# Two convolutions and a joint layer on one core: the order of the first loads, a split first tap and a wider leading tile

## The chip, the core and the metric

The kernel runs on one core of one Trainium2 chip. The metric is the device time of one execution in microseconds. A core has TensorE (PE) for matmuls, with its weight loads shown apart (PEld), VectorE (DVE), ScalarE (ACT), GpSimd (POOL) and SyncE (SP), which issues the DMA loads and stores of this kernel. Sixteen DMA engines move the data. Each engine runs its own instructions in order; semaphores tie them together.

## The reference

```python
B, T, D, K = 2, 4000, 512, 5          # x: (B, T, D); w1, w2: (K, D, D); g: (B, 8, D)
xp = jnp.pad(x, ((0,0),(pad,pad),(0,0)))
for i in range(K):
    h = h + jnp.einsum("btc,cd->btd", xp[:, i:i+T, :], w1[i])
h = _gelu(h)[:, ::2, :]
...                                    # the same with hp = pad(h) and w2
f = _gelu(f)[:, ::2, :]
fe = jnp.einsum("btd,de->bte", f, w_f)
ge = jnp.einsum("bud,de->bue", g, w_g)
j = jnp.tanh(fe[:, :, None, :] + ge[:, None, :, :])
return jnp.einsum("btud,dv->btuv", j, w_o)
```

Two convolutions of five taps, each with a GELU and a stride of 2, take 4,000 time steps to 1,000. Then every step is paired with 8 vectors of g, and the tanh of the sums goes through a last matmul. All data are bf16. Since only every second output of the first convolution is kept, an output column needs even samples for the even taps (0, 2, 4) and odd samples for the odd taps (1, 3).

## The kernel before, in words

**The leading tile.** The first 2 x NA output columns of the first convolution (NA = 216, line 328) are computed directly, tap by tap. Their samples come untransposed by `load_xr` (line 445) in two loads, one of 128 rows and one of NA + 2 - 128 = 90 rows; a row is four samples of 512 channels, 4,096 bytes. PE transposes them (line 501) into four PSUM banks, and four copies bring them into `xs`: DVE copies those of the first load, ACT those of the second. `direct(i, m)` (line 683) then runs one tap's 4 matmuls for one group of 128 output channels: 2 x NA = 432 columns each. The taps are taken in the order 0, 4, 2, 1, 3: 5 x 4 x 4 = 80 matmuls. They accumulate in PSUM banks 0 to 3, and a GELU on ACT ends them (line 693). Eight matmuls on zeros (`NWARM`, line 491) run on PE before the transposes.

**The triples.** The rest of the first convolution, and all of the second, is done in `Triple` (line 554): a fast scheme that makes three outputs from nine products, in place of more in the direct way. Its inputs are sums and differences of six phases of x (tiles `xq` and `xp`, loaded transposed by `load_x6`, line 449), made by DVE and ACT into `row`, and sums of the weights (`w1part`, line 534), made by DVE and ACT into `w_t` and `w_x`. The first triple's matmuls have N3 = 262 columns, and so have the second's; the others have 334. The leading tile has 72 triple positions of the 334 per batch (NA / 3), and the first two triples 131 each.

**What sets the order.** `Plan` (line 68) collects the operations. Up to line 694 they are pinned, so that each engine takes them in the order in which they are written. Behind that a list scheduler orders DVE and ACT by its own costs, among what is ready; PE, SP and POOL keep the written order among what is ready. Semaphore waits follow from the tiles that an operation reads and writes. `o.after` adds a wait by hand.

**SP's queue.** All loads stand on SP: xr (two), tap 0 of w1 in two halves by output columns (512-byte runs), taps 4, 2, 1 and 3 of 512 KB each, then the transposed loads of xq (twelve), of xp, and so on. Line 469 makes a w1 load wait until the load three places before it in the list `came` has landed. The transposed loads stand behind these waits.

**Weights on DVE.** `w1part(0)` begins with the first operation on w1 that the profile shows on DVE; it reads taps 0 and 4. The fourth operation on DVE reads tap 2, and the tenth taps 1 and 3 (line 543). The `row` operations of the first triple follow, and wait for the first two loads of xq.

The functions that the diff touches follow.

Of the kernel before, what the change touches and what calls it, by code (L numbers as in the profile page):

```python
# [7 lines left out]
ACT = mybir.ActivationFunctionType  # L8
# [4 lines left out]
P = 128  # L13
# [37 lines left out]
class Psum:  # L51
# [6 lines left out]
    def pair(self, lo, step, n):  # L58
        ap = self.h[:, lo:lo + 2 * step].rearrange("p (s c) -> p s c", s=2)[:, :, 0:n]
        cells = np.unique(np.concatenate([np.arange(lo, lo + n), np.arange(lo + step, lo + step + n)]) // 512)  # L60
        return View(ap, cells, True)
# [240 lines left out]
def bass_standalone__seq2seq_rnn_t_joint__speech_kernel(  # L302
# [33 lines left out]
    NWARM = 8  # L336

    with ExitStack() as es:
# [33 lines left out]
        xq = [Buf(nc, f"xq{i}", [6, NK, 288], BF16, v.end - v.bytes) for i, v in enumerate((xs[1], w2_sb))]  # L372
# [46 lines left out]
        def mm(o, pairs, start, stop, check=True):  # L419

            def fn(e):
                for n, (l, r) in enumerate(pairs):
                    ins = e.matmul(o.ap, lhsT=l.ap, rhs=r.ap, start=start and n == 0,  # L423
                                   stop=stop and n == len(pairs) - 1, skip_group_check=not check)
                return ins
            pl.op("pe", fn, [v for pr in pairs for v in pr], (o,), len(pairs) * max(o.ap.free_size() / 2400 + 0.0025, 0.1))
# [18 lines left out]
        def load_xr(rt):  # L445
            n = NR[rt]
            dst = xr[rt].rows(0, n).map(lambda a: a.rearrange("p r k c -> p (r k c)"))
            src = x[0, 4 * P * rt:4 * (P * rt + n), :].rearrange("(p r) c -> p (r c)", r=4)
            return pl.dma("sp", lambda e: e.dma_start(dst.ap, src), (), (dst,), nbytes=n * 4 * 2 * D)

        def load_x6(buf, b, ph, j0, col, n=336):
# [4 lines left out]
            pl.dma("sp", lambda e: e.dma_start_transpose(out=dst.ap, in_=src), (), (dst,), nbytes=n * 2 * D, rate=170e3)  # L456

        came = [load_xr(rt) for rt in range(2)]
        act(warm[0:1], warm[1:2], ACT.Gelu_apprx_tanh)

        def load_w1(i):
            src = w1[i].rearrange("(k c) d -> c k d", c=P)
            if len(came) == 2:
                h = D // 2
                for sl in (slice(0, h), slice(h, D)):
                    o = pl.dma("sp", lambda e, sl=sl: e.dma_start(w1_sb[i, :, sl].ap, src[:, :, sl]), (), (w1_sb[i, :, sl],), nbytes=262144)
            else:
                o = load_w("sp", w1_sb[i], src)
                o.after.append(came[-3].idx)
            came.append(o)  # L470

        def load_xq(i, ph):
            load_x6(xq[i], 0, ph, 2 * NA // 3 + i * N3 - 2, 0, -(-(N3 + 3 - i) // 16) * 16)

        for kind, i in (('w', 0), ('w', 4), ('w', 2), ('w', 1), ('w', 3), ('x', 4), ('x', 0), ('x', 2), ('x', 1), ('x', 3), ('x', 5)):
            if kind == "w":
                load_w1(i)
            else:
                load_xq(0, i)
        for ph in (4, 0, 2, 1, 3, 5):  # L480
            load_xq(1, ph)
# [8 lines left out]

        warm_mm(NWARM)
        psb = ps.h[:, :].bitcast(BF16)
        for rt in range(2):
            for pp in range(2):
                bk, n = 4 + 2 * pp + rt, NR[rt]
                pv = View(psb[:, bk * 1024:(bk + 1) * 1024].rearrange("p (r k c) -> p r k c", r=2, k=NK)[:, :, :, 0:n], np.array([bk]), True)

                def fn(e, rt=rt, pp=pp, pv=pv, n=n):
                    for r in range(2):
                        for k in range(NK):  # L500
                            ins = e.transpose(pv.ap[:, r, k, :], xr[rt].h[0:n, 2 * r + pp, k, :], ident.h[0:n, 0:n])
                    return ins
                pl.op("pe", fn, (xr[rt].rows(0, n), ident[:]), (pv,), 0.55)
                o = xs[0][pp::2, :, 16 + rt * P:16 + rt * P + n]
                if rt:
                    act(o, pv, ACT.Copy)
                else:
                    pl.op("dve", lambda e, o=o, pv=pv: e.tensor_copy(out=o.ap, in_=pv.ap), (pv,), (o,), vec_cost(o, (pv,)))
# [152 lines left out]
        trip = [Triple(xq[0], 2, row[0], wa, to_h(0, j3, N3), N3), Triple(xq[1], 2, row[1], wa, to_h(0, j3 + N3 // 2, N3), N3),  # L661
# [5 lines left out]
        for b in range(B):  # L667
            memset(hT[b][4:6, :, HOFF - 1:HOFF])
            memset(hT[b][:, :, HOFF + NT3:HOFF + NT3 + 2])
        memset(xq[1][0:4, :, 1 + N3:4 + N3])  # L670
        memset(xq[1][4:6, :, N3:4 + N3])
# [4 lines left out]
        def both(i, k):  # L676

            a, b = (xs[0][r, k, 16 + d:16 + d + NA] for r, d in tap_at[i])
            lo, hi = a.ap, b.ap
            ap = bass.AP(tensor=lo.tensor, offset=lo.offset, ap=[list(lo.ap[0]), [hi.offset - lo.offset, 2], [1, NA]])  # L680
            return View(ap, np.union1d(a.cells, b.cells), False)

        def direct(i, m):
            mm(ps.cols(m * NT, 2 * NA), [(w1_sb[i, k, m * P:(m + 1) * P], both(i, k)) for k in range(NK)],
               i == taps[0], i == taps[-1])

        for i in taps:
            for m in range(NK):
                direct(i, m)
        for m in range(NK):  # L690
# [436 lines left out]
```

## Time and profile before

| | us |
|---|---|
| median of 3 runs | 253.12 (252.08 to 253.51) |
| span of the profiled execution, first to last instruction | 251.3 |
| PE busy in the span | 245.7 (98%) |
| DVE busy | 211.8 (84%) |
| ACT busy | 210.5 (84%) |

The span is that of one profiled execution; its time by the clock of the runs is not listed by itself, and the median of the runs is 1.8 us above the span. "Busy" of PE counts matmuls that overlap in its pipeline, so the distance between two starts says more than the length of one.

The first loads, from the trace's records of issue and landing (us from the start of the span):

| load | issued | landed |
|---|---|---|
| xr, 128 rows | 0.74 | 4.17 |
| xr, 90 rows | 1.19 | 5.86 |
| w1 tap 0, two halves | 1.69, 2.14 | 6.61, 7.44 |
| w1 tap 4 | 4.19 | 8.94 |
| w1 tap 2 | 5.88 | 10.44 |
| w1 tap 1 | 7.46 | 12.42 |
| w1 tap 3 | 8.96 | 14.40 |
| xq, first and second of twelve | 9.37, 11.51 | 15.49, 17.94 |

In the first 10 us PE ends its transposes' stream at 6.93 and starts the direct taps at 7.47, when the copies of the even samples are there. In the profile a line such as `7.47 14.81 PE L423 MATMUL ...` gives the start, the length, the engine, the line of the kernel (L423 is the helper `mm`, L410 the helper `tt`, L456 the transposed load), what is written and read, and in brackets the idle time before it with what ended it.

### The profile page before, as it was taken

Reading aid. Unit: us, or ns where it says so; the run is one execution under the profiler, and the core shown is the slowest. Engines: PE = TensorE matmul, PEld = TensorE weight load, DVE = VectorE, ACT = ScalarE, POOL = GpSimd, SP = SyncE. Lnnn points to the kernel's source line nnn. Section 1 sums busy time; section 2 is a strip of 40 time slices with the busy share of each in tenths; the row PEclk is TensorE's granted clock in tenths of the full one; section 3 lists DMA queues with packets and bytes.
Section 4 is the critical chain, followed back from the end, with each engine's and each line's share of the span. In section 5 each row is a group of like instructions: output and inputs, shape, how many; then the busy total and the mean of one; then the engine's idle time right before and its main releaser. Section 6 shows DMA issues by size and latency. Waiting matters only on the chain.

```text
span 251.3 us, 5205 instructions
## 1 busy us (share of the span) xinstructions
PE 245.7 (98%) x1920; PEld 184.6 (73%) x1920; DVE 211.8 (84%) x347; ACT 210.5 (84%) x353; POOL 106.7 (42%) x109
## 2 busy tenths in 40 slices
PE   8999999999999999999999999999999999999994
PEld 4556788877666666666467878777788888778873
DVE  1699999967999997971547798999999999999892
ACT  2388699878959869963799999999999999997763
POOL 1000000000000000003338899698998999699930
PEclk9999999999999999999999999999999999999999
DMA  7999999988400052000002223322344336534648
GB/s 212 326 174 176 186 156 208 176 144 274 148 0 3 0 182 71 1 1 3 0 1 85 83 86 127 127 86 83 127 132 164 128 120 219 187 123 148 207 137 266
DMA packets 57392, 31.92 MB, mean 127 GB/s; under 512 B 33837, under 2 KB 57149, under 8 KB 57367
## 3 DMA queue, kind: packets, MB, share of 16 engines
q1 hardware_dynamic: 57367, 31.59, 48.0%
q8 instruction: 15, 0.25, 0.4%
q14 instruction: 10, 0.08, 0.1%
HBM read 7.71 MB, written 16.38 MB: 96 GB/s over the span
## 4 chain that ended last, share of the span: by engine, by line
PE 85%; DMA 6%; DVE 5%; ACT 2%; SPq 1%; issue 1%; DVEq 0%
PE acc L423 85%; DMA xq<-in_x_dram 3%; DMA w_sb<-in_w_dram 2%; DVE row L410 2%; DMA xr<-in_x_dram 1%; DVE xq L410 1%; SPq L456 1%; ACT sn L843 1%; DVE og L410 0%; ACT jT L415 0%; DVE sn L844 0%; DVE ssum L511 0%; ACT ost L843 0%; DVE w_t L410 0%; DVE w_x L410 0%
## 5 line engine op out<-in xcount | busy, mean ns | idle before, releaser
L410 DVE TENSOR_TENSOR og<-acc,sn 128x512 bf16<-128x512 f32 x87 | 56.9, 681 | 3.9 <-PE acc L423 3.1
L415 ACT ACTIVATE jT<-feT,geT 128x1000 bf16<-128x1000 f32 (+6 forms) x56 | 51.7, 975 | 0.5 <-DVE feT L736 0.4
L423 PE MATMUL acc<-tw,ss 128*128 128x256 f16 x348 | 48.0, 273 | 0.0
L912 POOL TENSOR_TENSOR ss<-jT 128x512 f16<-128x512 bf16 x28 | 33.8, 1219 | 12.9 <-ACT jT L415 10.6
L423 PEld LDWEIGHTS acc<-tw,ss 128*128 128x128 f16 x348 | 33.5, 98 | 7.3 <-DVE sn L844 0.3
L843 ACT ACTIVATE sn<-acc 128x512 f32<-128x512 f32 x52 | 31.5, 620 | 3.5 <-PE acc L423 3.2
L423 PE MATMUL acc<-row,w_sb 128*128 128x334 bf16 (+1 forms) x192 | 33.1, 295 | 0.2 <-DVE row L410 0.2
L423 PE MATMUL acc<-wo_sb,jT 128*128 128x256 bf16 (+1 forms) x196 | 31.7, 288 | 0.0
L407 POOL MEMSET hT<- 128x8 bf16 (+2 forms) x6 | 0.7, 148 | 71.8 <-ACT hT L415 66.8
L423 PE MATMUL acc<-row,w_x 128*128 128x262 bf16 (+1 forms) x192 | 28.2, 290 | 0.0
L415 ACT ACTIVATE jX<-feT,geT 128x1000 bf16<-128x1000 f32 (+4 forms) x28 | 25.0, 932 | 0.0
L423 PEld LDWEIGHTS acc<-row,w_sb 128*128 128x128 bf16 x192 | 18.5, 98 | 6.8 <-DVE row L410 0.5
L423 PEld LDWEIGHTS acc<-wo_sb,jT 128*128 128x128 bf16 x196 | 19.2, 98 | 5.3
L423 PEld LDWEIGHTS acc<-row,w_x 128*128 128x128 bf16 x192 | 18.8, 98 | 5.4
L415 ACT ACTIVATE sd<-acc 128x334 f32<-128x334 f32 (+1 forms) x48 | 20.5, 431 | 1.9 <-PE acc L423 1.3
L912 POOL TENSOR_TENSOR ss<-jX 128x512 f16<-128x512 bf16 x18 | 20.9, 1176 | 1.2 <-ACT jX L415 0.7
L415 ACT ACTIVATE hT<-acc 128x262 bf16<-128x262 f32 (+2 forms) x36 | 15.1, 432 | 6.7 <-PE acc L423 6.6
L511 DVE SCALAR_TENSOR_TENSOR acc<-acc,sd 128x334 f32<-128x334 f32 (+1 forms) x24 | 11.6, 483 | 10.4 <-PE acc L423 10.3
L844 DVE COPY sn<-acc 128x512 f32<-128x512 f32 x25 | 16.9, 682 | 2.4 <-PE acc L423 2.2
L423 PE MATMUL acc<-wo_sb,ss 128*128 128x256 bf16 x116 | 17.9, 273 | 0.0
L423 PE MATMUL acc<-hT,w_sb 128*128 128x334 bf16 x96 | 17.4, 305 | 0.0
L912 POOL TENSOR_TENSOR ss<-ss,jT 128x512 f16<-128x512 f16 x14 | 16.4, 1181 | 0.7 <-PE acc L423 0.4
(105 smaller groups left out, 501.6 us busy)
## 6 DMA issues: line engine op xcount, KB each, us to landing
out_dram<-og SPq DMA_DIRECT2D x44, 256.0 KB, 2.3
w_sb<-in_w_dram SPq DMA_DIRECT2D x9, 512.0 KB, 5.0
out_dram<-og SPq DMA_DIRECT2D x14, 128.0 KB, 2.7
out_dram<-ost SPq DMA_DIRECT2D x7, 128.0 KB, 2.0
xr<-in_x_dram SPq DMA_DIRECT2D x1, 512.0 KB, 3.4
w_sb<-in_w_dram SPq DMA_DIRECT2D x2, 256.0 KB, 5.1
wf_sb<-in_w_f_dram SPq DMA_DIRECT2D x1, 512.0 KB, 3.6
wg_sb<-in_w_g_dram SPq DMA_DIRECT2D x1, 512.0 KB, 4.7
```

Source lines behind the costliest of these rows:

```text
L407: pl.op("pool", lambda e: e.memset(v.ap, 0.0), (), (v,))
L410: pl.op(eng, lambda e: e.tensor_tensor(out=o.ap, in0=a.ap, in1=b.ap, op=op), (a, b), (o,), 0.02 + 2.14e-3 * o.ap.free_size() if eng == "po ...
L415: pl.op("act", lambda e: e.activation(o.ap, i.ap, func, scale=scale, bias=0.0 if bias is None else bias.ap), rd, (o,), o.ap.free_size() * ...
L423: ins = e.matmul(o.ap, lhsT=l.ap, rhs=r.ap, start=start and n == 0, stop=stop and n == len(pairs) - 1, skip_group_check=not check)
L456: pl.dma("sp", lambda e: e.dma_start_transpose(out=dst.ap, in_=src), (), (dst,), nbytes=n * 2 * D, rate=170e3)
L511: pl.op(eng, lambda e: e.scalar_tensor_tensor(out=o.ap, in0=a.ap, scalar=f, in1=b.ap, op0=ALU.mult, op1=add), (a, b), (o,), vec_cost(o, (a ...
L843: pl.flex({"act": (lambda e: e.activation(o.ap, v.ap, ACT.Copy), 0.05 + n * 0.833e-3), "dve": (lambda e: e.tensor_copy(out=o.ap, in_=v.ap) ...
L844: "dve": (lambda e: e.tensor_copy(out=o.ap, in_=v.ap), 0.065 + n * 1.04e-3)}, (v,), (o,))
L912: fn = lambda e, o=S[i], x=x, y=y, op=op: e.tensor_tensor(out=o.ap, in0=x.ap, in1=y.ap, op=op)
```

## The change

- `load_xr` is split by even and odd samples: each load takes two of the four samples of a row, in 1,024-byte runs. The order on SP becomes: even samples of the first rows, tap 0 in halves by input channels (1,024-byte runs), even samples of the second rows, tap 4, odd samples of both, taps 2, 1 and 3, and then the transposed loads as before. The waits by `o.after` are now: tap 2 for tap 4, tap 1 for the first odd samples, tap 3 for the second odd samples.
- NA is 228 in place of 216, so the second xr loads have 102 rows and the direct matmuls 456 columns; N3 is 258 in place of 262 for both triples.
- Tap 0 is done in two column parts (128 and 100 of each of the two interleaved output sets), and the first part in two halves of the input channels. Each part's accumulation covers both sets with `Psum.pair`.
- The transposes are taken apart in `turn`: those of the first even samples follow 5 warm-up matmuls and are followed by one more; those of the second even samples stand after the first 8 matmuls of tap 0; those of the odd samples stand between taps 4 and 2. DVE copies the even samples, ACT the odd ones.
- The memsets of hT and xq move in POOL's written order, and the planner's cost of a short matmul is lower (0.06 for 0.1 us).

The core of the diff (its changes to `Psum.pair` and to the sizes of xq are left out):

```diff
-    NA, N3 = 216, 262
+    NA, N3 = 228, (258, 258)
...
-    NWARM = 8
+    NWARM = 5
...
-        def load_xr(rt):
+        def load_xr(rt, pp):
             n = NR[rt]
-            dst = xr[rt].rows(0, n).map(lambda a: a.rearrange("p r k c -> p (r k c)"))
-            src = x[0, 4 * P * rt:4 * (P * rt + n), :].rearrange("(p r) c -> p (r c)", r=4)
-            return pl.dma("sp", lambda e: e.dma_start(dst.ap, src), (), (dst,), nbytes=n * 4 * 2 * D)
+            dst = xr[rt].rows(0, n, slice(pp, 4, 2)).map(lambda a: a.rearrange("p r k c -> p r (k c)"))
+            src = x[0, 4 * P * rt:4 * (P * rt + n), :].rearrange("(p r) c -> p r c", r=4)[:, pp::2, :]
+            return pl.dma("sp", lambda e: e.dma_start(dst.ap, src), (), (dst,), nbytes=n * 2 * 2 * D)
...
+        def load_w1(i, parts=1):
+            n = NK // parts
+            for k in range(0, NK, n):
+                src = w1[i, k * P:(k + n) * P].rearrange("(k c) d -> c k d", c=P)
+                dst = w1_sb[i, k:k + n]
+                o = pl.dma("sp", lambda e, dst=dst, src=src: e.dma_start(dst.ap, src), (), (dst,), nbytes=n * 131072)
+                if len(came) > 4:
+                    o.after.append(came[-3].idx)
+                came.append(o)
+
+        came = [load_xr(0, 0)]
+        load_w1(0, 2)
+        came.insert(2, load_xr(1, 0))
         act(warm[0:1], warm[1:2], ACT.Gelu_apprx_tanh)
...
+        load_w1(4)
+        for rt in range(2):
+            came.append(load_xr(rt, 1))
+        for i in (2, 1, 3):
+            load_w1(i)
...
+        def turn(rt, pp, eng):
+            bk, n = 4 + 2 * pp + rt, NR[rt]
...
+            def fn(e):
+                for r in range(2):
+                    for k in range(NK):
+                        ins = e.transpose(pv.ap[:, r, k, :], xr[rt].h[0:n, 2 * r + pp, k, :], ident.h[0:n, 0:n])
+                return ins
...
         warm_mm(NWARM)
...
+        turn(0, 0, "dve")
+        warm_mm(1)
...
+        for q0, n in ((0, P), (P, NA - P)):
+            for ks in ((0, 1), (2, 3)):
+                for m in range(NK):
+                    mm(ps.pair(m * NT + q0, NA, n), [(w1_sb[0, k, m * P:(m + 1) * P], both(0, k, q0, n)) for k in ks],
+                       q0 == 0 and ks[0] == 0, False, False)
+                if q0 == 0 and ks[0] == 0:
+                    turn(1, 0, "dve")
+        for i in taps[1:]:
+            if i == 2:
+                turn(0, 1, "act")
+                turn(1, 1, "act")
+            for m in range(NK):
+                direct(i, m)
```

More of the change, by code (lines that the diff above doesn't have):

```diff
@@ L371, in bass_standalone__seq2seq_rnn_t_joint__speech_kernel @@
         assert all(xp[i].end <= xs[i].end for i in xp)
-        xq = [Buf(nc, f"xq{i}", [6, NK, 288], BF16, v.end - v.bytes) for i, v in enumerate((xs[1], w2_sb))]
+        XQ = [-(-(N3[i] + 3 - i) // 16) * 16 for i in range(2)]
+        xq = [Buf(nc, f"xq{i}", [6, NK, XQ[i] + 16], BF16, v.end - v.bytes) for i, v in enumerate((xs[1], w2_sb))]
         assert xq[0].end <= xs[1].end and xq[1].end <= w2_sb.end
@@ L669, in bass_standalone__seq2seq_rnn_t_joint__speech_kernel @@
             memset(hT[b][:, :, HOFF + NT3:HOFF + NT3 + 2])
-        memset(xq[1][0:4, :, 1 + N3:4 + N3])
-        memset(xq[1][4:6, :, N3:4 + N3])
-        tap_at = {0: ((2, -1), (0, 0)), 1: ((3, -1), (1, 0)), 2: ((0, 0), (2, 0)),
-                  3: ((1, 0), (3, 0)), 4: ((2, 0), (0, 1))}
-        taps = (0, 4, 2, 1, 3)
[L676 to L689, printed above, removed]
         for m in range(NK):
```

69 lines of the change are left out of this document (30 added, 39 removed).

## The prediction, on record before the changed kernel ran

> **What bounds the kernel now.** I read the page's chain first: what ends last, and from when. Its header, and then its first 30 us as the chain view gives them (start, length, what):
>
> ```profile
> PE 85%; DMA 6%; DVE 5%; ACT 2%; SPq 1%; issue 1%; DVEq 0%
> ```
>
> ```profile
> 0.74 3.43 DMA xr<-in_x_dram
> 4.17 0.02 issue
> 4.19 4.75 DMA w_sb<-in_w_dram
> ...
> 9.37 2.09 SPq L456
> 11.46 0.05 issue
> 11.51 6.42 DMA xq<-in_x_dram
> 17.94 0.02 issue
> 17.96 1.29 DVE row L410 x2
> ...
> 28.17 0.61 DVE row L410
> 28.78 0.05 issue
> 28.83 185.64 PE acc L423 x1464
> ```
>
> From 28.83 us on TensorE (PE) is the bound without a break for 185.64 us. Before that the chain does not run through PE: it goes through loads (xr, w1, the second transposed load of xq, landing at 17.94) and then through VectorE (DVE), which makes the operands of the triples. The change touches only what happens before 28.83 us and the size of some later matmuls. So the question is when DVE now lets PE go. The timeline of PE and DVE in that stretch (start, length, engine, line, operation):
>
> ```profile
> 1.19 3.60 PE L423 MATMUL acc<-zero 128*128 128x512 bf16 x8 [1.19 <-DVE zero L430]
> 7.47 14.81 PE L423 MATMUL acc<-xs,w_sb 128*128 128x432 bf16 x80 [0.54 <-ACT xs L415]
> 8.97 0.69 DVE L511 SCALAR_TENSOR_TENSOR ssum<-w_sb 128x512 f32<-128x512 bf16 x1 [1.96 <-DMA w_sb<-in_w_dram]
> 10.78 0.68 DVE L511 SCALAR_TENSOR_TENSOR ssum<-w_sb,ssum 128x512 f32<-128x512 bf16 x1
> 17.96 0.70 DVE L410 TENSOR_TENSOR row<-xq 128x1048 bf16<-128x1048 bf16 x1 [0.43 <-DMA xq<-in_x_dram]
> 28.83 0.62 PE L423 MATMUL acc<-row,w_sb 128*128 128x262 bf16 x4 [0.20 <-DVE row L410]
> ```
>
> DVE starts on w1 when tap 4 has landed (8.97), needs tap 2 first in the operation at 10.78, and from there to 17.53 it runs 11 operations back to back, one per 0.605 us. It idles 0.43 us for xq, then works without a pause to 28.78. PE, in contrast, is nearly level: 80 matmuls from 7.47 to 22.12 (0.183 us apart), then 56 of 262 columns at 0.1105 us, to 28.35, then it waits for DVE. An earlier start of the direct taps is therefore worth next to nothing by itself: DVE's chain must come earlier too.
>
> **Own time.** The span is 251.3 us and the median of the three runs 253.12, so 1.8 us lies around it. I make the sum as a shift of the span and add it to 253.12.
>
> **Part 1, the start on PE.** xr's first load lands at 4.17 with 8 packets of 4,096 B per DMA engine, 0.16 us each in the packet records. The even half is half of that: 0.64 us earlier, 3.55. Five warm-up matmuls at 0.427 us end at 3.3. The 8 transposes and the copy took 4.58 to 6.37 in before (5.675 + 0.69); moved to 3.65 they end at 5.44. PE starts tap 0 at 5.45, not 7.47: 2.0 us earlier. Its work from there: 16 matmuls of 256 columns, 16 of 200 and 64 of 456, at 0.183 us scaled by columns (0.109, 0.085, 0.1935): 15.5 us; 24 transposes now behind the start, at the 0.056 and 0.044 us that they show once fast: 1.15 us. 5.45 + 16.65 = 22.1, as now (22.12). The earlier start is eaten by 24 more columns in every matmul and by the transposes. The 56 matmuls then end at 28.3 at best.
>
> **Part 2, the loads.** This is where the time goes. The trace's packet records end each load in 4-byte packets, one per engine that it ran on: the 128-row xr load has 16, the 90-row one 15. The output stores, of 8 to 128 rows, have 1,486 in all, exactly the sum of each one's largest divisor of its rows up to 16; 16 each would be 1,552. With the tile at 228 columns the second xr load has 102 rows (2 x 3 x 17): its two halves go through **6 engines**, 34 packets of 1,024 B each, against 13 if all 16 shared them.
>
> The price of a packet: tap 4 lands at 8.94, tap 2 at 10.44, so 32 packets per engine in 1.5 us, 0.047 us each (the next two loads took 2.0 us each, 0.062, the other end). On those six engines, in queue order from xr's even half at 3.55: tap 0's halves 16 packets each, 4.3 and 5.05; xr1 even 34, 6.65; tap 4 32, 8.15; xr0 odd 8.9; xr1 odd 10.5; tap 2 12.0; tap 1 13.5; tap 3 15.0. The gap from last packet to landing grows from 0.5 us in the first load to 0.75 in the next, so add 0.25: tap 4 8.4 (now 8.94), **tap 2 12.25 (now 10.44)**, tap 3 15.25 (now 14.40). The other ten engines run dry meanwhile: SP holds tap 2 until tap 4 has landed.
>
> No row tells which six engines. Ends: the same six twice (68 packets where 26 would be even, 42 x 0.047 = 2.0 us behind), or two different sixes (half of it). I take the same six, since nothing in the records moves on from load to load, and keep the other as a rival.
>
> The Trainium skill, DMA: Bandwidth & Descriptors, section "Why a DMA increments its semaphore by 16 and not by 1", says that a load uses the largest count up to 16 that divides both sides' slowest dimension, and on the hardware queues always the lowest-numbered engines. The first half agrees with the 15 and the 1,486 above; the second half no row shows. By it both halves sit on the same six, the end I took.
>
> **Part 3, SP.** Tap 3 is now issued behind a wait for xr1's odd half (10.75 landed). Behind it on SP stand all transposed loads: xq's first issue goes from 9.37 to 10.75 + 0.4 = 11.15, 1.8 us later, and its second landing from 17.94 to 19.75. Lower end: that load's issue took 2.8 us where most took 1.6; if it sheds this, 18.55.
>
> **Part 4, DVE.** Its operation at 10.78 now waits for tap 2, 12.27; 11 operations later it is 19.0 (tap 3, needed at 15.9, is there). The first row operation starts at the later of 19.0 and xq (18.55 to 19.75): 19.0 to 19.75 against 17.96; I take **+1.6** (19.55), nearer to the unshortened issue. From there to PE's release stand the same 18 operations, 12 of them 1.5% narrower (about 0.01 us each): -0.1. Release at 28.83 + 1.5 = 30.3. PE would be there at 28.75 (22.1, plus 0.5 waiting for xr1 even, which lands at 6.9 when PE is ready at 6.3, plus 56 x 0.110).
>
> ScalarE now does the odd copies (0.77 + 0.69 us) between weight work; the third doubled row, behind one 1.04 us weight copy, ends near 22.7, before DVE asks for it at 23.2. Cost nothing; without that cover at most 0.5. The unpinned order behind is otherwise the same up to swaps of neighbours, and the moved memsets fill tiles that trip 1 and the second convolution read after 30 us: nothing.
>
> **Part 5, later matmuls.** Triples 0 and 1 have 288 matmuls of 258 columns in place of 262; 232 come after the release: 232 x 4 columns x 0.42 ns (0.183 us / 432) = -0.4 us, straight off the bound.
>
> **Sum:** +1.6 - 0.1 - 0.4 = **+1.1 us, 254.2**; by the ends +0.5 to +2.0 (slow packets), 253.6 to 255.1.
>
> **Rivals.**
> - *The loads are spread evenly* (not slower). 13 packets per xr1 half: tap 4 7.4, tap 2 10.25, xr1 odd 8.75, xq's issue 9.15. DVE passes 10.25 where it stood at 10.78, ends at 17.0 and waits for xq at 17.7: -0.25 - 0.1 - 0.4 = -0.75, **252.4**. It decides if tap 2 lands before 10.8. Against it: 102 has no divisor from 7 to 16, and the store counts. Chance 0.12.
> - *Two different sixes.* Tap 2 near 11.7, xq's issue near 10.1: +0.7 - 0.5 = **253.3**. Chance 0.11.
> - *PE stays slow for longer.* Row: matmuls in before start 0.427 us apart, transposes 0.107, until 5.86, and from there at twice the pace, 4.7 us after the first matmul, with PE never idle (the page's granted clock reads full all along and does not show this). In after PE idles at 3.3 to 3.6 and 4.9 to 5.45. Each slow us costs 0.5; PE has 1.6 us of cover under DVE (28.75 to 30.3) and 0.5 in the wait for xr1, so it decides once the slow pace lasts 4.2 us longer, to 10.1. If counting starts anew at 5.45 it ends at 10.15: hidden. If it lasts until 13: 3.6 - 2.1 = +1.5, **255.7**. Chance 0.15.
>
> The Trainium skill, TensorE: Matmul & The Clock Gate, Part 1, says that PE runs at half rate until one free-running window of about 3.4 us was busy. The 4.7 us agree. By it the pace doubles between 8.9 and 12.3 if the idle spots spoil the windows before: nothing at the one end, +1.1 at the other.
>
> **Numbers.** Forecast 0.62, the rivals 0.12, 0.11, 0.15. Half a per cent, about what a measurement of this kernel can tell from no change, is 1.27 us: 251.85 to 254.39. Of the forecast's 0.62 (253.6 to 255.1, spread by the runs' own 1.4 us) 0.29 lie above; with the third rival and a trace of the second that is 0.46 slower. Faster: a good half of the even-spread case, 0.07. Within: 0.47. Range: below, it reaches into the even-spread case, 252.6; above, to the slow-PE case, 255.9.
>
> **What would show it.** Right: tap 0's first matmul near 5.5; the first DVE operation on w1 near 8.4, its fourth waiting for w_sb until about 12; xq's first issue near 11; row operations from about 19.5; PE's unbroken stretch from about 30.3. Wrong: xq's first issue before 10 (the loads were spread), or matmuls of 456 columns still 0.38 us apart after 10 us (PE slow).

## The result, and the profile after

| | before | changed |
|---|---|---|
| median of 7 runs each, us | 253.12 (252.08 to 253.79) | 256.38 (254.58 to 257.15) |
| ratio of the two | | 1.0121, 95% interval 1.0095 to 1.0147 |
| profiled execution: its time, span | -, 251.3 | 254.67, 252.9 |

The change makes the kernel 3.3 us slower. The forecast was 254.2, and the range ended at 255.9: the sign of the sum was right, its size was not. The profiled execution is one of the two fastest of the changed kernel: its 254.67 us lie inside the forecast's range, and its trace shows less of the loss than a usual run has. Part of the difference is visible: before's trace has some 0.9 us of stalls on PE at 214 to 222 us that this one lacks. Of the 18 traces of the experiments below, 16 have these stalls too (all but those of kernels 9 and 15), so a usual run of the changed kernel probably has them; no trace shows it. From 54 to 210 us (in before's time), ahead of these stalls, every matmul of the changed kernel comes 2.86 to 2.89 us later than its counterpart in before, the matmuls counted from the end. The start, which the trace does show, thus makes up 2.9 of the 3.3 us.

The chain of waits of the changed kernel (header, then start, length, what):

```profile
PE 95%; DMA 2%; SPq 1%; ACT 0%; issue 0%
```

```profile
2.63 5.90 DMA xr<-in_x_dram
8.53 0.04 issue
8.57 0.86 PE acc L504 x8
9.43 6.43 PE acc L425 x40
15.86 0.81 PE acc L504 x16
16.67 233.36 PE acc L425 x1848
```

In before this chain ran through loads and DVE until 28.83 us. Now it is one load and then PE alone: the second even samples land at 8.53, and from 8.57 on nothing but PE holds the end. The timeline of PE, and then of DVE:

```profile
5.71 1.05 PE L425 MATMUL acc<-xs,w_sb 128*128 128x256 bf16 x8 [0.57 <-DVE xs L511]
8.57 0.86 PE L504 MATMUL acc<-ident,xr 102*128 102x102 bf16 x8 [1.81 <-DMA xr<-in_x_dram]
9.23 6.64 PE L425 MATMUL acc<-xs,w_sb 128*128 128x256 bf16 x40
16.51 9.43 PE L425 MATMUL acc<-xs,w_sb 128*128 128x456 bf16 x48
25.78 4.16 PE L425 MATMUL acc<-row,w_x 128*128 128x258 bf16 x36
```

```profile
14.21 0.69 DVE L518 SCALAR_TENSOR_TENSOR ssum<-w_sb,ssum 128x512 f32<-128x512 bf16 x1 [2.24 <-DMA w_sb<-in_w_dram]
21.40 0.70 DVE L412 TENSOR_TENSOR row<-xq 128x1032 bf16<-128x1032 bf16 x1 [0.47 <-DMA xq<-in_x_dram]
```

PE does eight matmuls early, idles 1.81 us for the second samples, and ends the direct taps at 25.78 (22.12 in before). DVE waits 2.24 us for tap 2 and has its first row operation at 21.40 (17.96). The table of windows (window, its length, busy time of PE, PEld, DVE, ACT and POOL, granted clock of PE, share of the DMA engines, GB/s) shows a mark of each delay:

```profile
5.00:6.50 1.50, 0.93 (x9) 0.70 (x8) 0.65 (x1) 0.00 (x0) 0.00 (x0) 1.00 0.39 117
6.50:8.00 1.50, 0.26 (x3) 0.00 (x0) 0.00 (x0) 0.00 (x0) 0.00 (x0) 1.00 0.99 316
8.00:9.50 1.50, 0.93 (x10) 0.87 (x11) 0.03 (x1) 0.00 (x0) 0.00 (x0) 0.53 0.77 246
9.50:11.00 1.50, 1.50 (x9) 1.06 (x8) 1.47 (x3) 0.00 (x0) 0.00 (x0) 0.50 0.35 108
```

From 5.0 to 6.5 us, while the 102-row load is on, the DMA engines are busy for 0.39, which is 6 of 16, although tap 4 and the odd samples' two loads were issued behind it, from 3.63 us on. In before the share in the same window is 1.20:

```profile
5.00:6.50 1.50, 1.50 (x24) 1.50 (x23) 0.82 (x2) 0.00 (x0) 0.00 (x0) 1.00 1.20 278
```

And PE's granted clock, which is 1.00 at full speed, is 0.5 from 8 to 11 us, behind the idle stretch.

Landing times and what hangs on them, as predicted and as measured (the last column is the kernel that closed the gap, below):

| us | before | predicted | changed | gap closed |
|---|---|---|---|---|
| second even samples landed | 5.86 (whole xr) | 6.9 | 8.53 | 6.64 |
| tap 4 landed | 8.94 | 8.4 | 10.06 | 8.13 |
| tap 2 landed | 10.44 | 12.25 | 14.12 | 11.14 |
| xq issued first | 9.37 | 11.15 | 12.71 | 8.56 |
| xq's second landed | 17.94 | 18.55 to 19.75 | 21.38 | 17.55 |
| first row operation on DVE | 17.96 | 19.55 | 21.40 | 17.86 |
| direct taps end on PE | 22.12 | 22.6 | 25.78 | 22.71 |

### The profile page after: what moved, and what is told of

It is laid out like the page before. It is cut to its first block, busy times and chain, and to the rows that moved or that the text cites. A ratio compares the mean times of both kernels' runs of the same rounds, so it can differ in the third digit from the quotient of the medians.

```text
span 252.9 us, 5239 instructions
## 1 busy us (share of the span) xinstructions
PE 246.0 (97%) x1934; PEld 186.2 (74%) x1934; DVE 210.1 (83%) x347; ACT 209.1 (83%) x353; POOL 106.8 (42%) x109
## 4 chain that ended last, share of the span: by engine, by line
PE 95%; DMA 2%; SPq 1%; ACT 0%; issue 0%
PE acc L425 95%; DMA xr<-in_x_dram 2%; PE acc L504 1%; SPq L465 0%; SPq L451 0%; ACT ost L417 0%
## 5 line engine op out<-in xcount | busy, mean ns | idle before, releaser
L425 PE MATMUL acc<-row,w_x 128*128 128x258 bf16 (+1 forms) x192 | 28.1, 289 | 0.0
L417 ACT ACTIVATE hT<-acc 128x258 bf16<-128x258 f32 (+2 forms) x36 | 15.4, 435 | 6.3 <-PE acc L425 6.3
L518 DVE SCALAR_TENSOR_TENSOR acc<-acc,sd 128x334 f32<-128x334 f32 (+1 forms) x24 | 11.5, 480 | 10.0 <-PE acc L425 10.0
L425 PE MATMUL acc<-xs,w_sb 128*128 128x456 bf16 (+2 forms) x96 | 17.1, 341 | 0.6 <-DVE xs L511 0.6
## 6 DMA issues: line engine op xcount, KB each, us to landing
out_dram<-og SPq DMA_DIRECT2D x44, 256.0 KB, 2.3
xr<-in_x_dram SPq DMA_DIRECT2D x2, 256.0 KB, 5.0
w_sb<-in_w_dram SPq DMA_DIRECT2D x2, 256.0 KB, 3.6
```

Of the source, the lines that this page charges most:

```text
L417: pl.op("act", lambda e: e.activation(o.ap, i.ap, func, scale=scale, bias=0.0 if bias is None else bias.ap), rd, (o,), o.ap.free_size() * ...
L518: pl.op(eng, lambda e: e.scalar_tensor_tensor(out=o.ap, in0=a.ap, scalar=f, in1=b.ap, op0=ALU.mult, op1=add), (a, b), (o,), vec_cost(o, (a ...
```

## The experiments

The theory after the result had two paths. **Loads**: the six-engine loads, and waits behind them, bring samples and weights late, so that PE and DVE both start late. **Pace**: PE loses its full pace in the idle stretches and does the first taps at half of it. The rival of each is the other one alone. Ratios are to before, run on the same chip at the same time; the kernels ran in groups on different chips, so the ratios compare across groups better than the medians do. The first columns are from one profiled execution each: when the transposes of the second even samples start, when tap 2 lands, when the direct taps end, the time between the first and the third of these (D), and the first row operation.

| kernel | transposes | tap 2 | taps end | D | row | median | ratio, interval |
|---|---|---|---|---|---|---|---|
| changed | 8.57 | 14.12 | 25.78 | 17.21 | 21.40 | 256.38 | 1.0121 (1.0095 to 1.0147) |
| 1: 112 rows | 8.59 | 14.35 | 26.64 | 18.05 | 21.07 | 255.28 | 1.0103 (1.0083 to 1.0124) |
| 2: before, 102 rows | - | 12.62 | 26.73 | - | 20.16 | 256.80 | 1.0165 (1.0146 to 1.0185) |
| 3: nine zeros, planned | 8.55 | 13.15 | 26.48 | - | 19.87 | 257.67 | 1.0199 (1.0169 to 1.0228) |
| 4: tile 216 | 9.13 | 14.65 | 25.86 | - | 21.38 | 255.23 | 1.0093 (1.0076 to 1.0110) |
| 5: 128 rows | 8.00 | 13.32 | 25.46 | 17.46 | 20.04 | 254.92 | 1.0077 (1.0047 to 1.0106) |
| 6: 128 rows, zeros | 8.04 | 13.54 | 23.86 | 15.82 | 20.27 | 254.55 | 1.0073 (1.0044 to 1.0102) |
| 7: loads as before | 9.33 | 11.14 | 25.83 | 16.50 | 19.18 | 256.45 | 1.0139 (1.0108 to 1.0169) |
| 8: tap 0 not split | 7.91 | 13.73 | 27.31 | - | 20.45 | 257.94 | 1.0203 (1.0174 to 1.0233) |
| 9: changed, zeros | 8.60 | 14.04 | 24.41 | 15.81 | 21.38 | 255.05 | 1.0109 (1.0076 to 1.0142) |
| 10: 128 rows, waits | 7.94 | 12.67 | 24.81 | 16.87 | 19.40 | 254.74 | 1.0078 (1.0041 to 1.0116) |
| 11: the same, zeros | 8.56 | 11.75 | 24.36 | 15.80 | 18.47 | 254.29 | 1.0070 (1.0043 to 1.0097) |
| 12: tap 0 in one load | 7.88 | 12.37 | 24.98 | 17.10 | 19.09 | 254.75 | 1.0084 (1.0053 to 1.0114) |
| **13: all of these** | 6.91 | 11.14 | 22.71 | 15.80 | 17.86 | **252.82** | **0.9988 (0.9975 to 1.0001)** |
| 14: 11, two zeros | 7.98 | 13.21 | 23.80 | 15.82 | 19.93 | 253.76 | 1.0028 (1.0014 to 1.0041) |
| 15: 13, odd samples later | 6.99 | 11.36 | 22.79 | 15.80 | 19.89 | 254.99 | 1.0070 (1.0044 to 1.0096) |
| 16: before, 5 warm-ups | - | 10.99 | 21.83 | - | 17.97 | 253.80 | 1.0027 (1.0009 to 1.0044) |
| 17: 13, 102 rows | 8.58 | 14.44 | 24.39 | 15.81 | 21.15 | 255.26 | 1.0105 (1.0062 to 1.0149) |
| 18: 13, no zeros | 6.94 | 11.38 | 22.74 | 15.80 | 18.10 | 254.71 | 1.0101 (1.0060 to 1.0141) |

D is 15.8 us wherever PE keeps its full pace, to within 0.02 in eight kernels; what is above that is half pace. The columns show the two paths: D and the transposes make PE's, tap 2 and the row operation make DVE's.

### The rows of the second xr load (1, 2, 4, 5)

```diff
             n = NR[rt]          # changed kernel: 102 rows
+            n = (P, 112)[rt]    # 1
+            n = P               # 5
+            n = (P, 102)[rt]    # 2, in the kernel before (it loads 90)
-    NA, N3 = 228, (258, 258)    # 4: the tile of before, and so 90 rows
+    NA, N3 = 216, (262, 262)
```

The added rows of 1 and 5 are loaded and not used.

> The changed kernel with one edit: the two loads of the second xr rows fetch 112 rows in place of 102 (ten rows that nothing reads). Theory A (a load of 102 rows runs on 6 DMA engines, and the loads issued behind it reach the other ten only when it is nearly through): 112 rows run on 16 engines, 14 packets each, so xr's second even half lands near 6.8 us in place of 8.5, the first xq load is issued before 10 us in place of 12.7, the direct taps end near 22.5 in place of 25.8, and the time is 252.3 to 253.7. Theory B (TensorE's half pace after its idle spots is what costs): the idle spot shrinks but stays, so at least half of the loss stays, 254.7 to 256.4.

> The kernel before with one edit: its second xr load fetches 102 rows in place of 90 (twelve rows that nothing reads), in 4,096-byte packets. Theory A: 6 engines with 17 packets of 0.16 us, 2.7 us, in place of 15 engines with 6, 1.0 us, and tap 0 behind it waits: all loads behind are 1.5 to 1.8 us later, and so is the time, 254.3 to 255.0. Theory B: twelve rows more are 48 KB, 0.15 us; the time is that of before, 252.8 to 253.5.

> The changed kernel with the old tile: 216 and 262 columns in place of 228 and 258, the rest of the change as it is. The second xr rows are 90 again and run on 15 engines. Theory A: no load holds the queue up; the first xq load is issued before 10 us and the time is 252.3 to 253.5. Theory B, or the new order itself being the cost: the order and the idle spots are those of the change, so the time stays over 255.

> The changed kernel with the second xr loads at 128 rows (26 rows that nothing reads): 16 engines with 8 rows each, as the first load has. The profile of the 112-row kernel still shows packets that stand for 0.3 to 0.9 us and engines without work between 5 and 7 us. Theory A1 (row counts that do not give each engine 8 whole rows cause these stops): xr's second even half lands near 6.5 us, and the time is 252.8 to 254.2. Theory C (the stops belong to the new order, seven loads at once and the odd halves ahead of tap 2): as with 112 rows, 254.8 to 255.5.

The 102 rows alone cost the kernel before 1.65%, the largest single effect of all. PE's timeline of that kernel:

```profile
8.30 1.38 PE L501 MATMUL acc<-ident,xr 90*128 90x90 bf16 x16 [2.90 <-DMA xr<-in_x_dram]
9.95 16.95 PE L423 MATMUL acc<-xs,w_sb 128*128 128x432 bf16 x80 [0.26 <-ACT xs L415]
```

xr's second load landed at 8.26 in place of 5.86, PE idled 2.90 us for it, and the 80 direct matmuls took 16.95 us in place of 14.81: both theories in one kernel. In the changed kernel the way back (5) is worth 0.0121 - 0.0077 = 0.0044, 1.1 us, with intervals that overlap a little; there the transposes come only 0.57 earlier. Kernel 4 has the tile of before and 15 engines, and its 1.0093 lies between 1 and 5, so the tile's width is not what costs. The profiled executions of 1 and 4 are the slowest of their kernels (256.65 and 256.69); in that of 4, two packets stood for 2.3 and 2.5 us while the second even samples were on their way. The packet records confirm the engines: up to 12.2 us the changed kernel has 92 of the 4-byte end packets, sixteen for each of five loads and six for each of the two 102-row loads, and kernels 1 and 5 have 112. But 16 engines alone did not do what was expected of them: with 112 rows the transposes start at 8.59 (8.57 in the changed kernel), and the times of 1, 4 and 5 all lie above the 252.3 to 254.2 us that were expected if the engines were the cost. Six engines are thus a cause, shown in the kernel before, and not the whole of it.

The Trainium skill, DMA: Bandwidth & Descriptors, section "Why a DMA increments its semaphore by 16 and not by 1", has a load run on the largest count up to 16 that divides its rows. The share of 0.39 for 102 rows agrees (6 of 16 is 0.375). That it is always the lowest-numbered engines is what no run here shows.

### Zeros on PE, and the planner in the way (3, 6, 9)

```diff
         warm_mm(NWARM)
+        warm_mm(1, 3, 0.0)
         turn(0, 0, "dve")
         warm_mm(1)
+        warm_mm(2, 3, 0.0)
...
                 if q0 == 0 and ks[0] == 0:
+                    warm_mm(6, 7, 0.0)      # 3: nine here, at the planner's cost of 0.43, and none above
                     turn(1, 0, "dve")
```

Matmuls on zeros into a bank that nothing uses then keep PE busy while it waits. 6 has 128 rows, 3 and 9 have 102. The new arguments of `warm_mm` are the PSUM bank and the cost that the planner is told.

> The changed kernel with nine more matmuls on zeros (512 columns, into a bank that is still free) between the first 8 matmuls of tap 0 and the transposes of the second even samples, so that TensorE does not idle while it waits for that load. Theory A: the loads stay as late as they are and VectorE's chain with them, so little is won: 255.4 to 256.5. Theory B: TensorE keeps its full pace from its first doubling on; 48 matmuls that ran at half pace no longer do, and the time falls by 1.4 us or more, to 253.5 to 255.0.

> The kernel with 128 rows, with nine more matmuls on zeros that the planner is told cost nothing, so that the order on all engines stays: one more before the first transposes, two after them, six after the first 8 matmuls of tap 0. TensorE then hardly idles between 1.2 us and the arrival of the second even samples. Theory B (half pace after idle spots is most of what is left): 0.8 to 2 us faster than the kernel with 128 rows alone. Theory A (the landing of the loads sets the end, through VectorE's chain): within 0.4 us of it.

> The changed kernel as it is (102-row loads), with nine matmuls on zeros between the early stretches of PE (one before the first transposes, two behind them, six behind the first eight matmuls of tap 0), none of them moving DVE's or ACT's order. Theory A (PE's half pace after its idle stretches is the cost that ends last): full pace from about 5 us on, the direct taps end 1.5 to 2.5 us earlier than in the changed kernel (near 23.7), and the time falls by 1.0 to 2.0 us, to 254.0 to 255.3. Theory B (the loads are late and DVE's chain is what ends last): PE gains the same, waits for DVE near 27 to 31 us instead, and the time stays within 0.6 us of the changed kernel, 255.6 to 256.8. The first row operation on DVE stays near 21.4 by both.

Kernel 3 was no test: with the zeros' cost in its plan, the scheduler put DVE's copy of the second even samples behind three weight operations (10.95 us), and PE waited for it until 11.58. With the cost at 0.0 the orders of DVE and ACT stay, and the pace is restored: D falls from 17.46 to 15.82 in 6, and from 17.21 to 15.81 in 9. But the ratios hardly move (1.0077 to 1.0073, 1.0121 to 1.0109, both within the intervals). The chain of kernel 9 tells where the 1.4 us went:

```profile
4.75 7.66 DMA xr<-in_x_dram
...
12.83 6.43 DMA xq<-in_x_dram
19.27 0.02 issue
19.29 1.07 ACT row L417
...
26.23 0.83 ACT sd L417 x3
27.06 12.96 PE acc L425 x115
```

PE now waits until 27.06 for a chain that the odd samples' 102-row load begins: SP cannot issue tap 3 and the xq loads behind it before 12.4 us, and ACT and DVE make the rows that late. So each path stood behind the other, and taking one away shows almost nothing. Kernel 9's 255.05 us lie in the range that was given for the pace alone, but its trace shows the wait at 27 us that was expected of the loads. Of the two theories neither alone is right.

### Order, waits and number of loads (7, 8, 10, 11, 12)

```diff
-        load_w1(0, 2)                    # 12: tap 0 as one load of 512 KB
-        came.insert(2, load_xr(1, 0))
+        load_w1(0)
+        came.append(load_xr(1, 0))
...
-                    o.after.append(came[-3].idx)
+                    o.after.append(came[{2: 3, 1: 2, 3: 4}[i]].idx)   # 10 and 11
...
-        for q0, n in ((0, P), (P, NA - P)):    # 8: tap 0 whole, behind both transposes
+        turn(1, 0, "dve")
+        for m in range(NK):
+            mm(ps.cols(m * NT, 2 * NA), [(w1_sb[0, k, m * P:(m + 1) * P], both(0, k)) for k in range(NK)], True, False, False)
```

All have 128 rows. In 10 and 11 tap 2 waits for tap 0's second half, tap 1 for the second even samples and tap 3 for tap 4; 11 has the zeros of 6. Kernel 7 keeps the changed kernel's order on PE with before's whole xr loads, ahead of all weights.

> The changed kernel with the load order of before: both xr loads whole and first (the second with 128 rows), tap 0 in two halves, then taps 4, 2, 1, 3, each behind the wait that it had in before; TensorE's order, the split tap 0 and the wide tile are those of the change. Theory C (the order of the loads is the cost): the first xq load is issued near 9.5 us, and the time is 252.0 to 253.4. Theory B (TensorE's side, idle spots and half pace, is the cost): it stays at 254.3 or more.

> The kernel with 128 rows, with tap 0 in one piece: TensorE starts it only when both even halves are copied, and the early start of the change is gone. If the early start is worth what its 2 us promise, 1 to 2 us slower than the kernel with 128 rows. If the loads set the end (theory A or C), within 0.5 us of it.

> The changed kernel with 128 rows in its second xr loads (so 16 end packets), and the three waits of the weight loads put one or two loads earlier: tap 2 waits for the second half of tap 0, tap 1 for the second even samples, tap 3 for tap 4. Theory B (the waits leave the DMA engines without work at 9 to 11.5 us and make DVE late): tap 2 lands near 11.6 in place of 13.3, xq's first issue falls near 9.8 in place of 11.2, DVE's first row operation comes 1.4 to 1.8 us earlier; the time by itself falls only as far as PE's half pace lets it, to 253.9 to 254.9. Theory A (only PE's half pace counts): DVE comes earlier all the same, but the time stays within 0.4 us of the 254.92 of the kernel with 128 rows. Third case: tap 2 then takes room from tap 4 and the odd samples, PE's taps come later, and the time is 255.2 or more.

> The last kernel (128 rows, waits earlier) and the nine matmuls on zeros together. If late weight loads and PE's half pace are the two costs, each with the other behind it, then this one loses both: direct taps end near 23.8, first row operation near 18.5, and the time is 252.5 to 253.4, no slower than before. If DVE's start is held by something else (xq's transposed loads, ACT's share of the weight sums), the time stays at 254.0 to 254.7, as with the zeros alone.

> The changed kernel with 128 rows in its second xr loads and tap 0 as one load of 512 KB in place of two of 256 KB (its matmuls stay split). If many short loads leave the DMA engines partly idle, the second even samples land near 6.5 to 7.0 (7.95 with two halves), PE starts a little later (6.2) but waits less, and the time falls to 253.8 to 254.6. If the number of loads is not what makes them late, the second even samples stay near 7.9, PE starts 0.6 us later and the time is 254.9 to 255.8.

Before's loads with the new order on PE (7) are no way back: PE has nothing between 5.6 and 7.67, and the second transposes stand behind the first eight matmuls although their samples landed at 5.45. The split of tap 0 by itself is good: without it (8) PE idles 2.46 us, and the time is 257.94 against 254.92 of kernel 5, run beside it. So the early start is worth 3.0 us by the medians (the direct taps of the two traces end 1.85 us apart) *within the new load order*; it repairs what that order does.

Earlier waits bring tap 2 from 13.32 to 12.67 and the rows from 20.04 to 19.40, less than half of what was expected, and the ratio does not move (1.0077, 1.0078). Kernel 11 was expected level with before, at most 253.4, and took 254.29: a miss. Its trace says that its samples landed at 7.30, but that PE was still at its six zeros until 8.5; the remedy held up what it was to protect. One load for tap 0 brings the second samples to 6.88, where two halves gave 7.30 to 8.00 in the six kernels with 128 rows (5, 6, 8, 10, 11, 14); but PE at half pace was still at its first eight matmuls until 7.9.

### All together, and each taken back (13, 14, 15, 17, 18)

Kernel 13 has 128 rows, tap 0 in one load, the earlier waits, and three zeros around the first transposes with none behind; 14 is kernel 11 with two zeros in place of six. Kernels 17 and 18 take back one part of 13 each: the rows, and the zeros. Kernel 15 is 13 with the odd samples' loads behind tap 2.

```diff
-            n = NR[rt]
+            n = P                                   # not in 17
...
-                if len(came) > 4:
-                    o.after.append(came[-3].idx)
+                if len(came) > 3:
+                    o.after.append(came[{2: 1, 1: 2, 3: 3}[i]].idx)
...
-        load_w1(0, 2)
-        came.insert(2, load_xr(1, 0))
+        load_w1(0)
+        came.append(load_xr(1, 0))
...
+        load_w1(2)                                  # 15, ahead of the odd samples
...
+        warm_mm(1, 0.0)                             # not in 18
         turn(0, 0, "dve")
         warm_mm(1)
+        warm_mm(2, 0.0)                             # not in 18
```

> The changed kernel with 128 rows in the second xr loads, tap 0 as one load, the weight loads' waits earlier (tap 2 waits for tap 0, tap 1 for the second even samples, tap 3 for tap 4) and three zeros on PE around the first transposes, none behind the first eight matmuls. If the landing of the second even samples plus 15.8 us of PE work at full pace is all that PE's side costs, and the weight loads all that DVE's side costs: samples landed near 6.9, their transposes start near 7.1, direct taps end near 22.9, first row operation near 18.0 to 18.5, and the time is 252.2 to 253.2, within half a per cent of before. If a third cost exists, the time stays at 253.8 or more although both are met.

> The kernel with 128 rows, earlier waits and zeros (254.29 us), with two zeros behind the first eight matmuls of tap 0 in place of six. If the four surplus zeros held PE (0.85 us at 0.213 each), the transposes of the second even samples start near 7.7 in place of 8.56 when they have landed by then, and the time falls by 0.5 to 0.9, to 253.4 to 253.8. If the samples land at 7.9 or later, or something else holds the start, it stays within 0.3 of 254.3.

> The kernel with tap 0 as one load, earlier waits and three zeros, with the two loads of odd samples put behind tap 2 in the queue. Two-path account: tap 2 lands near 10 in place of 11, DVE's operation on it starts as early as in before (10.8) or earlier, the first row operation then waits for xq near 17.5 to 18; PE's release is held by PE itself near 29.0, and the time is 252.0 to 253.0, level with the kernel that keeps the odd samples ahead, or up to 0.5 less. If the odd samples come too late for PE's third tap (transposes behind 13), it is 253.5 or more.

> The kernel that closed the gap (tap 0 as one load, earlier waits, three zeros, 252.82 us), with 102 rows again in its second xr loads, so six end packets. If the six engines hold up the queue by themselves: second even samples near 7.9 in place of 6.6, tap 4 and all behind it 1.5 to 2.5 us later, and the time is 254.0 to 255.2. If with earlier waits the ten other engines find work all the same, it stays within 0.5 us of 252.8.

> The kernel that closed the gap without its three zeros (PE then idles some 0.5 us before the first transposes and 0.8 us before tap 0), order of DVE and ACT the same. If idle stretches of that length bring PE's half pace back: tap 0 at twice the spacing until 9 to 11 us, direct taps 1.0 to 1.5 us later than 22.7, and the time is 253.6 to 254.4. If the pace needs longer idle stretches to fall, nothing changes: 252.6 to 253.1.

PE's timeline and two windows of kernel 13:

```profile
6.91 0.52 PE L504 MATMUL acc<-ident,xr 102*128 102x102 bf16 x8
7.27 5.53 PE L425 MATMUL acc<-xs,w_sb 128*128 128x256 bf16 x40
22.71 3.68 PE L425 MATMUL acc<-row,w_x 128*128 128x258 bf16 x32
```

```profile
5.00:6.50 1.50, 1.50 (x8) 0.64 (x7) 0.69 (x1) 0.00 (x0) 0.00 (x0) 1.00 1.09 375
9.50:11.00 1.50, 1.50 (x11) 0.82 (x9) 0.55 (x1) 0.00 (x0) 0.00 (x0) 1.00 1.10 351
```

PE is busy without a break, the forty matmuls take 5.53 us in place of 6.64, and the DMA engines are full at 1.09 and 1.10 where the changed kernel had 0.39 and 0.35. The time is that of before: 252.82 against 253.02, ratio 0.9988. No third cost is needed to explain the gap. What the change was built from gains nothing beyond before even when both costs are gone: 0.2 us, and the interval of the ratio includes 1. No kernel takes back the earlier waits, or the one load for tap 0, alone, so their shares in 13 are not shown.

Taking back the rows (17) costs 1.0105 against 0.9988, 3.0 us: the second transposes come at 8.58, tap 2 at 14.44, and the chain runs through xq and ACT again. PE keeps its pace there (D 15.81), so this is the loads' part by itself. It does not come from empty engines: their share is 0.77 from 5.0 to 6.5 us and 1.09 from 6.5 to 8.0. It is the narrow load itself that takes long: in 13 the second even samples land 0.74 us after tap 0 (5.90, 6.64), and in 17 PE still waits for them 2.2 us after tap 0 has landed (6.38, 8.58). Taking back the zeros (18) costs 1.0101, 2.9 us by the ratios. But its profiled execution shows nothing of it:

```profile
6.06 1.04 PE L425 MATMUL acc<-xs,w_sb 128*128 128x256 bf16 x8 [0.73 <-DVE xs L511]
22.74 3.68 PE L425 MATMUL acc<-row,w_x 128*128 128x258 bf16 x32
```

PE idled 0.73 us and came out of it at full pace; that execution took 253.11, and the five others 254.48 to 257.05. That the others lost the pace fits kernel 13's narrow spread (252.09 to 253.12) beside this one's, but no trace shows them: it is argued, not shown. The two prices, 3.0 and 2.9 us, together exceed the changed kernel's gap of 3.3, as they would where two paths lie side by side and the longer one sets the end.

Kernel 14 fell to 253.76, as expected for fewer zeros, though its samples landed at 7.94, where no gain was expected. Kernel 15 missed: tap 2 was issued at 6.04 with little in the queue, landed at 11.36, no earlier than in 13, and the scheduler put three more weight operations ahead of the first row operation (19.89). It says nothing clean about the odd samples' place.

### Five warm-ups in the kernel before (16)

```diff
-    NWARM = 8
+    NWARM = 5
```

> The kernel before with five warm-up matmuls in place of eight, and nothing else. If an idle stretch of about 1 us on PE (3.3 to 4.2) starts the count of its slow pace anew, the transposes and tap 0 run at half pace until about 9 in place of 5.9, the direct taps end about 1 us later (23.1), 0.5 us of it hidden behind DVE: 253.1 to 253.7. If the pace depends only on the time since PE's first matmul, full pace comes at 5.9 as before and nothing changes: 252.3 to 253.0.

The ratio is 1.0027 (1.0009 to 1.0044): a small cost, 0.7 us. The profiled execution idles 0.67 us before the transposes, does the 80 direct matmuls in 14.81 us as before does, and lies within 0.03 us of before from 36 us on; its 253.28 is among the three fastest of eleven. As in 18, the loss is in runs that no trace shows.

## Why the prediction was wrong, point by point

**What bounds, right in kind.** That the gain of an early start is eaten, that the 102 rows mean six engines, and that tap 2, SP's queue and DVE's chain come late was all seen, and the sign of the sum with it.

**Part 1, right.** Tap 0 was to start at 5.45 and started at 5.71.

**Part 2, the step that failed first.** The second even samples were to land at 6.9, by 34 packets at 0.047 us behind tap 0's; they landed at 8.53, 1.63 us later. The landings split this: the first load came at 3.95 in place of 3.55 (0.40), tap 0's halves took 1.83 us more in place of 1.5 (0.33), and the six-engine load took 2.75 us (5.78 to 8.53) where the sum has 1.6 (1.15), less the 0.25 that the sum added for the landing. So the term that was mis-sized most is the six-engine load itself, at 34 x 0.047. A part of that is not the six engines: with 128 rows and tap 0 in halves (5, 6, 8, 10, 11, 14) the samples still landed only at 7.30 to 8.00, and the engines ran partly empty (0.79 from 5.0 to 6.5 us in kernel 5). Why they do so between small loads, no run shows. The prediction also saw the other ten engines run dry only by SP's wait for tap 2; here they were dry from 5 to 6.5 us with tap 4 already issued (0.39). Everything behind inherits the delay: tap 4 +1.7, tap 2 +1.9, against the landings forecast.

**Parts 3 and 4, right in mechanism, mis-sized by the same term.** xq's first issue came at 12.71 (11.15), its second landing at 21.38 (19.75), the first row operation at 21.40 (19.55). That the later of tap 2's eleven operations and xq decides was right: DVE was free at 20.9 and waited 0.47 us for xq. DVE's path alone is some 1.9 us later than forecast.

**Part 4's cover, the other failed step.** "PE would be there at 28.75", 1.6 us ahead of DVE. PE ended the direct taps at 25.78 where 22.6 was forecast: 8.57 - 6.95 = 1.6 us by the samples, 17.21 - 15.80 = 1.4 us by half pace, and 0.2 us by which the forecast's own sum was short of 6.95 + 15.80. With that PE has no cover but is itself the bound, and the chain shows nothing else from 8.57 on.

**The third rival was half right.** It named PE's slow pace, let it matter from 10.1 us on, and with an end at 13 gave 255.7. The pace doubled near 11.5 (the granted clock is 0.83 in the window from 11.0 to 12.5). It mattered because the cover was gone, and it came from an idle stretch (1.81 us) that the rival had not counted, since it let PE wait only 0.5 us for the samples. Its mechanism and the forecast's came together, while they had been priced as alternatives, each with the other's good case. The range therefore had no room for both: the lag of 2.87 us that they left is more than twice the forecast's 1.1, and added to 253.12 it gives 256.0, past the range's end at 255.9. What a usual run loses beyond that, no trace shows.

**What brings the half pace back.** The length of an idle stretch alone does not tell. Stretches of 1.81 us (changed kernel), 1.27 us (kernel 5) and 2.90 us (kernel 2) brought it back after PE had been at full pace, with the granted clock at 0.50 to 0.60 in the windows behind the first two; 1.62 us in kernel 3 did not, nor did 0.48 to 0.89 us in kernels 9, 14, 15, 17 and 18. In narrower windows the granted clock is 0.50 from 8.09 to 11.51 us in the changed kernel, from 8.29 to 11.70 in kernel 5 and from 7.51 to 14.34 in kernel 2: 3.41 us, once, once and twice. In the 3.41 us ahead of these PE was busy for 1.51, 1.63 and 1.30 us. In kernel 3 the 3.41 us that hold the stretch (8.87 to 12.28, in steps from 5.46, where its clock record begins) have PE busy for 1.79 us, and the clock stayed at 1.00. So the busy share of such a stretch of 3.41 us seems to decide; four cases are few, and this is argued, not shown. Where full pace had not been reached before the first taps (1, 4, 10, 12), these began slow behind idle stretches of 0.36 to 0.82 us. The Trainium skill, TensorE: Matmul & The Clock Gate, Part 1, has PE fall back to half rate after an idle window of about 3.4 us, one that runs free of the kernel. The 3.41 us agree with that window; that a whole idle one is needed does not hold here, and the measurement decides.

**Part 5, right.** From 36 us to 65 (in before's time), the stretch in which most of the 232 narrower matmuls lie, the lag falls from 3.14 to 2.86; 167 matmuls x 4 columns x 0.42 ns give 0.28.

**The other rivals.** An even spread of the loads is refuted by the end packets, 92 where 16 engines for every load would leave 112, and by the share of 0.39. Whether the halves ran on the same six engines or on two different sixes, no view shows: tap 2 at 14.12 is far from both sums (12.25 and 11.7).

**What stays open.** Why a usual run of the changed kernel takes 1.7 us more than its profiled one (the stalls of 0.9 us at 214 to 222 us may be a part); what the longer executions of kernels 15, 16 and 18 do; why a load of 112 rows on 16 engines came as late as one of 102 on six; and why two loads of 256 KB hold up what follows by about 1 us more than one of 512 KB.

## What to carry to other kernels

When two paths are level to within a microsecond, price a change for both at once and let their delays meet: a cover worked out from the good case of one path is no cover, and an experiment that mends one path alone will look like a failed theory. Count the engines that each load gets from its rows, and expect a narrow load, and what is queued behind it, to land late; padding the rows from 102 to 128, unused, cost nothing that shows and was worth 1.1 to 3.0 us here (padding to 112 showed no clear gain). Moving work forward in front of a load that it then waits for makes an idle stretch, and on PE that was paid twice here: 1.81 us of waiting, and 1.4 us of half pace behind it.

## What the hardware showed that was not expected

- A load on six engines lands late and makes what follows late: in kernel 17 tap 4 landed at 9.98 in place of 8.13 and tap 2 at 14.44 in place of 11.14. In the changed kernel and kernel 9 the share of busy DMA engines meanwhile fell to 0.39 from 5.0 to 6.5 us with tap 4 issued behind it; in kernel 17 it was 0.77, so the empty engines are not the whole of it.
- A wait in the load queue must be over well before the queue is empty. Tap 2 of kernel 5 was issued at 9.40, when tap 4 had landed, and landed 3.9 us later, while loads that keep the engines full follow each other at 1.5 us; the share from 9.5 to 11.0 was 0.32. In kernel 15 an issue at 6.04 was still too late to keep the engines full (0.68 from 7.5 to 8.0).
- PE's half pace came back in the middle of the start and lasted 3.41 us (the changed kernel and kernel 5) or twice that (kernel 2), with a granted clock of 0.50. The granted clock reads 1.00 in kernel 12, whose forty matmuls took 6.50 us in place of 5.53; the trace's clock record begins only at 10.56 us there, just where the spacing of equal matmuls falls from 0.17 to 0.09 us. Ahead of that record the spacing is the only sign.
